# Four-head logit bursts, softmax normalisation in token layout, and an instruction order from a list scheduler, in a two-layer attention and feed-forward kernel

## The chip, the cores and the metric

The kernel runs on one core of a Trainium2 chip. The metric is the device time of one execution in microseconds (us). A run more than 1.5% above the fastest of its kernel counts as slow.

The engines are PE (matrix multiply; PEld is its weight load), DVE (vector), ACT (activation), POOL (general purpose) and SP (here only a queue that issues DMAs). "PEclk" is the TensorE clock that the throttle granted, as a share of full speed.

## The reference, cut to what matters

```python
def _A_ref(x, wq, wk, wv, wo, beta):        # S 2048, D 512, H 32 heads of Dh 16, N 4 segments of L 512
    ...                                      # q, k, v per head and segment
    phi = lambda t: jnp.where(t > 0, t + 1.0, jnp.exp(t))
    g = _sigmoid(beta).reshape(1, H, 1, 1)
    for s in range(N):
        logits = einsum('bhqd,bhkd->bhqk', qs, ks) * scale + mask      # causal inside the segment
        a_dot = einsum('bhqk,bhkd->bhqd', softmax(logits), vs)
        pq = phi(qs)
        a_mem = einsum('bhld,bhde->bhle', pq, M) / (einsum('bhld,bhd->bhl', pq, z)[..., None] + 1e-06)
        outs.append(g * a_mem + (1.0 - g) * a_dot)
        pk = phi(ks)
        M = M + einsum('bhld,bhle->bhde', pk, vs);  z = z + einsum('bhld->bhd', pk)
    ...
    return o @ wo

def _B_ref(x, w1, w3, w2):                   # F = 1376
    return (silu(x @ w1) * (x @ w3)) @ w2

x = x + _A_ref(layernorm(x), ...);  x = x + _B_ref(layernorm(x), ...)      # twice, the same weights
```

With 16 channels a head, the logits use only a small part of the PE's rows, so several heads are run side by side in row groups ("row-tiled"); the products with V are run side by side in column groups ("column-tiled"); projections and the feed-forward part (FFN) use the full array. Changing from one form to another is called a mode change below.

## The kernel before

A small scheduler orders the instructions of each engine ahead of time with durations that the author wrote down; the order in the program is then fixed, and engines wait for each other by semaphores. It takes, engine by engine, the instruction that can start earliest, with program order breaking ties. Program order itself interleaves attention with "fillers", the FFN of the previous segment:

```python
# schedule(): among the pending operations of engine e
if cand is None or ready < cand_ready - 1e-9:
    cand, cand_ready = op, ready
if ready <= tf + 1e-9:
    break
# ... cut ...
def run_interleaved(main_gen, ratio=2):
    for _ in main_gen:                     # one quad (four heads) of attention,
        for _r in range(ratio):            # then two pieces of FFN
            if fillers: ...
```

Logits are computed for two heads at a time, two exponentials per unit, and the value product follows each unit:

```python
for ui, blocks in enumerate(QUNITS):       # 3 units for each quad of heads
    for half in range(2):
        pgs = (2 * half, 2 * half + 1)     # two row groups of four
        # lg_fn: for each block and each pg of pgs: one 32-row matmul
        S.add("pe", lg_fn, ..., writes=hres)
        S.add("act", ... Ebuf[:, 2*half:2*half+2, 0:NT_] = exp(Sl4[:, 2*half:2*half+2, 0:NT_]))
    # pool: affine_select masks; pe: ad_fn, the value product, column-tiled, into ONE bank Xb
```

The output of each quad is channel-major in PSUM. DVE transposes it, and the memory term, out of PSUM, and normalises there; then transposes the whole back:

```python
S.add("dve", ... e.transpose(ST[:, 0], Xb[:, 0:512]))        # attention
S.add("dve", ... e.transpose(ST[:, 1], Yb[:, 0:512]))        # memory, from the nd4 matmuls
... reciprocals, gates ...
otb = ST0 * r0;  oslot = ST1 * r1;  oslot += otb             # three DVE products, 256 columns each
S.add("dve", ... e.transpose(oT[0][:, G, :], ost))           # back, once for two quads
```

The softmax here doesn't subtract the row's maximum and nothing guards it: scores larger than these inputs give would overflow.

## Time and profile before

728.47 us median of 4 runs (727.32 to 729.45). The profiled run has a span of 726.4 us.

| before | PE | DVE | ACT | POOL | idle PE | granted clock |
|---|---|---|---|---|---|---|
| whole span, 726.4 us | 582.2 | 527.7 | 444.7 | 206.5 | 144.2 | 0.908 |
| 160 to 480 us | 264.9 | 237.7 | 201.0 | 90.5 | 55.1 | 0.93 |

The page's busy line, then PE's busy tenths in 40 slices of 18.2 us and the granted clock in tenths, then the chain of work that ended last, by engine:

```profile
PE 582.2 (80%) x4192; PEld 203.4 (28%) x4192; DVE 527.7 (73%) x1178; ACT 444.7 (61%) x586; POOL 206.5 (28%) x292
...
PE   0776897889958888788958899588987898988497
...
PEclk9986569899979999899988999789998999899889
...
PE 41%; DVE 37%; ACT 8%; DMA 6%; issue 4%; SPq 2%; POOL 1%; POOLq 0%; DVEq 0%
```

No engine is full, and the chain passes from PE to DVE and back: it is a kernel in which engines wait for each other. The timeline of PE in the middle shows how (start, duration, engine and line, operation, in the brackets the idle time before it and what ended it). L531 is logits, L553 values, L565 the memory read, L678 and L682 the FFN:

```profile
231.30 0.40 PE L553 MATMUL psall<-Ebuf,Vaug 128*32 128x512 bf16 x4 [0.55 <-DVE ST L575]
231.65 0.34 PE L531 MATMUL psall<-qT,kTm_0 32*128 32x256 bf16 x4
231.92 1.04 PE L682 MATMUL psall<-xnT,w 128*128 128x512 bf16 x4
232.79 1.03 PE L678 MATMUL psall<-xnT,w 128*128 128x512 bf16 x4
233.75 0.35 PE L553 MATMUL psall<-Ebuf,Vaug 128*32 128x384 bf16 x4
...
234.97 0.40 PE L565 MATMUL psall<-phiQ,Maug 32*32 32x512 bf16 x4 [0.54 <-DVE ST L578]
235.30 0.39 PE L531 MATMUL psall<-qT,kTm_1 32*128 32x512 bf16 x2
236.14 1.04 PE L682 MATMUL psall<-xnT,w 128*128 128x512 bf16 x4 [0.46 <-DVE pb L687]
```

Each burst is short, the modes alternate (687 mode changes in the built order), and small waits for DVE are spread between them.

The last view has three stretches of 8 us and one of 30: from and to, length, busy time of PE, PEld, DVE, ACT and POOL with their instructions, granted clock, DMA share, GB/s. In the two stretches where PE is busy 40% and 37% of the time the clock is 0.55 and 0.50, and where it is busy 81% the clock is 1.00. But from 75 to 105 us PE is busy 89% and the clock is 0.50 all the same:

```profile
200.00:208.00 8.00, 3.20 (x25) 0.74 (x26) 7.90 (x16) 4.71 (x5) 3.98 (x4) 0.55 0.39 80
232.00:240.00 8.00, 6.45 (x54) 2.27 (x55) 6.33 (x15) 6.12 (x9) 2.58 (x4) 1.00 0.00 0
376.00:384.00 8.00, 2.96 (x18) 0.84 (x19) 1.72 (x4) 3.48 (x5) 2.70 (x5) 0.50 0.48 98
75.00:105.00 30.00, 26.84 (x179) 6.14 (x180) 13.54 (x28) 26.80 (x35) 14.23 (x23) 0.50 0.00 1
```

The Trainium skill ("TensorE: Matmul & The Clock Gate", Part 1) says that an idle PE is granted half speed and gets full speed after about 3.4 us of sustained work. This trace agrees as to the two levels: 0.50 and 0.55 in the dry stretches, 1.00 in the dense one. It does not agree as to the time: the clock stays at half from 75 to 105 us with PE busy for 26.8 of these 30 us, from 78.48 to 82.88 us without a pause.

### The profile page before, as it was taken

The page shows a single profiled execution, that of the slowest core. Times are in us where ns is not written, and L with a number is a line of the kernel's source. Part 1 is how long each engine was busy: PE and PEld are TensorE (multiplying, and loading weights), DVE is VectorE, ACT ScalarE, POOL GpSimd, SP SyncE. Part 2 cuts the span into 40 slices and gives each one's busy share as a digit, 9 for nine tenths or more (in the row PEclk, how much of TensorE's full clock was granted, in tenths as well). Part 3 has the DMA queues.
Part 4 walks back from the last instruction along what each step waited for, and adds up shares of the span by engine and source line. Part 5 has one row for each costly group of instructions (what it writes and reads, how often), then busy time and mean ns, then how long its engine had stood idle before and what let it go on. Part 6 is the DMA issues. An engine that isn't in the chain of part 4 may idle for free.

```text
span 726.4 us, 10730 instructions
## 1 busy us (share of the span) xinstructions
PE 582.2 (80%) x4192; PEld 203.4 (28%) x4192; DVE 527.7 (73%) x1178; ACT 444.7 (61%) x586; POOL 206.5 (28%) x292
## 2 busy tenths in 40 slices
PE   0776897889958888788958899588987898988497
PEld 0221222223312333223312233122332232223143
DVE  7647468978777778977865677777778869877654
ACT  0658989674657757677475846567476764675020
POOL 3314443331233323232321312223223233222000
PEclk9986569899979999899988999789998999899889
DMA  5933001300040000300021000300012001000200
GB/s 174 289 89 59 1 1 29 59 1 1 1 85 4 1 1 8 81 1 1 0 51 39 0 1 6 80 5 1 1 37 52 1 1 45 15 1 1 54 4 30
DMA packets 56931, 23.81 MB, mean 33 GB/s; under 512 B 52544, under 2 KB 55120, under 8 KB 56880
## 3 DMA queue, kind: packets, MB, share of 16 engines
q1 hardware_dynamic: 54912, 15.22, 9.9%
q0 software_dynamic: 1968, 7.91, 3.3%
q8 instruction: 33, 0.54, 0.3%
q14 instruction: 18, 0.15, 0.1%
HBM read 8.43 MB, written 2.10 MB: 14 GB/s over the span
## 4 chain that ended last, share of the span: by engine, by line
PE 41%; DVE 37%; ACT 8%; DMA 6%; issue 4%; SPq 2%; POOL 1%; POOLq 0%; DVEq 0%
PE psall L678 8%; PE psall L682 8%; PE psall L701 8%; DMA xnT<-xn 5%; ACT Ebuf L539 5%; DVE ST L575 5%; DVE pb L687 4%; PE psall L553 4%; PE psall L531 4%; PE psall L628 3%; DVE ST L578 3%; DVE hT L690 3%; DVE ostage L617 2%; DVE phiK L491 2%; DVE otmp L611 2%
## 5 line engine op out<-in xcount | busy, mean ns | idle before, releaser
L539 ACT ACTIVATE Ebuf<-psall 128x768 bf16<-128x768 f32 (+1 forms) x384 | 317.4, 885 | 66.7 <-PE psall L531 66.2
L544 POOL TENSOR_SCALAR_AFFINE_SELECT Ebuf<-Ebuf 128x512 bf16<-128x512 bf16 x256 | 180.0, 704 | 385.7 <-ACT Ebuf L539 381.3
L685 ACT ACTIVATE sgb<-psall 128x512 bf16<-128x512 f32 (+1 forms) x88 | 52.5, 597 | 111.4 <-PE psall L678 111.4
L678 PE MATMUL psall<-xnT,w 128*128 128x512 bf16 (+1 forms) x352 | 99.7, 409 | 18.0 <-DMA xnT<-xn 17.6
L682 PE MATMUL psall<-xnT,w 128*128 128x512 bf16 (+1 forms) x352 | 102.6, 408 | 6.3 <-DVE pb L687 5.2
L575 DVE STREAM_TRANSPOSE ST<-psall 128x512 f32<-128x512 f32 x64 | 45.6, 712 | 72.5 <-PE psall L553 72.4
L553 PE MATMUL psall<-Ebuf,Vaug 128*32 128x512 bf16 (+3 forms) x1024 | 75.8, 333 | 19.0 <-DVE ST L575 14.8
L687 DVE SCALAR_TENSOR_TENSOR pb<-sgb,psall 128x512 bf16<-128x512 bf16 (+1 forms) x88 | 58.6, 665 | 35.3 <-PE psall L682 20.0
L701 PE MATMUL psall<-w,hT 128*128 128x512 bf16 (+1 forms) x352 | 81.0, 380 | 2.0 <-DVE x_tok L705 1.5
L531 PE MATMUL psall<-qT,kTm_1 32*128 32x128 bf16 (+3 forms) x512 | 65.4, 332 | 9.4 <-ACT Ebuf L539 9.2
L531 PE MATMUL psall<-qT,kTm_0 32*128 32x256 bf16 (+3 forms) x512 | 63.4, 330 | 10.3 <-ACT Ebuf L539 10.0
L690 DVE TENSOR_TENSOR hT<-pb,psall 128x512 bf16<-128x512 bf16 (+1 forms) x88 | 59.7, 678 | 1.0
L466 ACT ACTIVATE qT<-psall 128x512 bf16<-128x512 f32 x32 | 19.3, 603 | 63.3 <-PE psall L450 63.3
L450 PE MATMUL psall<-xnT,wq 128*128 128x512 bf16 x128 | 36.3, 403 | 26.3 <-DMA xnT<-xn 26.0
L678 PEld LDWEIGHTS psall<-xnT,w 128*128 128x128 bf16 (+1 forms) x352 | 33.4, 104 | 68.1 <-DMA xnT<-xn 19.5
L682 PEld LDWEIGHTS psall<-xnT,w 128*128 128x128 bf16 (+1 forms) x352 | 31.5, 105 | 53.2 <-DVE pb L687 16.6
L565 PE MATMUL psall<-phiQ,Maug 32*32 32x512 bf16 x192 | 21.3, 435 | 31.2 <-DVE ST L578 25.4
L553 PEld LDWEIGHTS psall<-Ebuf,Vaug 128*32 128x32 bf16 x1024 | 21.0, 95 | 87.8 <-issue 43.8
L701 PEld LDWEIGHTS psall<-w,hT 128*128 128x128 bf16 (+1 forms) x352 | 32.5, 98 | 44.2 <-DVE x_tok L705 5.4
L628 PE MATMUL psall<-wo,oT 128*128 128x512 bf16 x128 | 37.4, 402 | 8.6 <-DVE oT L620 5.2
L427 DVE TENSOR_SCALAR xn<-x_tok,lnmv 128x512 bf16<-128x512 bf16 x64 | 28.2, 475 | 21.2 <-DMA xnT<-xn 17.3
L416 DVE BATCH_NORM_STATS2 lnst<-x_tok 128x6 f32<-128x512 bf16 x64 | 42.0, 674 | 0.3
(72 smaller groups left out, 604.7 us busy)
## 6 DMA issues: line engine op xcount, KB each, us to landing
w<-in_B_w_dram POOLq DMA_DIRECT2D x2, 1376.0 KB, 13.1
out_dram<-x_tok SPq DMA_DIRECT2D x4, 512.0 KB, 2.9
x_tok<-in_A_x_dram POOLq DMA_DIRECT2D x3, 512.0 KB, 7.0
w<-in_B_w_dram POOLq DMA_DIRECT2D x1, 1280.0 KB, 17.6
xnT<-xn SPq DMA_TRANSPOSE x64, 2.5
x_tok<-in_A_x_dram SPq DMA_DIRECT2D x4, 128.0 KB, 2.9
wq<-in_A_wq_dram POOLq DMA_DIRECT2D x1, 512.0 KB, 4.7
wk<-in_A_wk_dram POOLq DMA_DIRECT2D x1, 512.0 KB, 5.6
```

Of the source, the lines that this page charges most:

```text
L531: ins = e.matmul(Sl4[:, pg, ecol:ecol + N], kTm[sp][ee][32 * pg:32 * pg + 32, G, 128 * j:128 * j + 128], qT[sp][32 * pg:32 * pg + 32, G, 1 ...
L539: S.add("act", lambda e, eslot=eslot, NT_=NT_, half=half: e.activation(Ebuf[eslot][:, 2 * half:2 * half + 2, 0:NT_], Sl4[:, 2 * half:2 * h ...
L544: S.add("pool", lambda e, eslot=eslot, ecol=ecol: e.affine_select(Ebuf[eslot][:, :, ecol:ecol + 128], Ebuf[eslot][:, :, ecol:ecol + 128], ...
L553: ins = e.matmul(Xb[32 * pg:32 * pg + 32, 128 * j:512], Vaug[sp][:, j, heads[pg], :], Ebuf[eslot][:, pg, ecol:ecol + N], start=(j == 0), s ...
L575: S.add("dve", lambda e, ST=ST: e.transpose(ST[:, 0, :, :].rearrange("p a r -> p (a r)"), Xb[:, 0:512]), reads=[xres], writes=[("ST", sts, ...
L628: S.add("pe", lambda e, i=i, G=G, pso=pso: e.matmul(pso, oT[0][:, G, 128 * i:128 * (i + 1)], wo_sb[:, G, :], start=(G == 0), stop=(G == NC ...
L678: S.add("pe", lambda e, cg=cg, f0=f0, fw=fw, gps=gps, b=b: e.matmul(gps[0:fw, :], w1_sb[:, cg, f0:f0 + fw], xnT[b][:, cg, :], start=(cg == ...
L682: S.add("pe", lambda e, cg=cg, f0=f0, fw=fw, ups=ups, b=b: e.matmul(ups[0:fw, :], w3_sb[:, cg, f0:f0 + fw], xnT[b][:, cg, :], start=(cg == ...
L685: S.add("act", lambda e, k3=k3, fw=fw, gps=gps: e.activation(sgb[k3][0:fw, :], gps[0:fw, :], ACT.Tanh, scale=0.5), reads=[gres], writes=[( ...
L687: S.add("dve", lambda e, k3=k3, fw=fw, ups=ups: e.scalar_tensor_tensor(pb[k3][0:fw, :], sgb[k3][0:fw, :], 1.0, ups[0:fw, :], ALU.add, ALU. ...
L690: S.add("dve", lambda e, k3=k3, fw=fw, ft=ft, gps=gps: e.tensor_tensor(hT[0:fw, ft, :], pb[k3][0:fw, :], gps[0:fw, :], ALU.mult), reads=[( ...
L701: S.add("pe", lambda e, ft=ft, fw=fw, i=i, dps=dps: e.matmul(dps[:, :], hT[0:fw, ft, 128 * i:128 * (i + 1)], w2_sb[0:fw, ft, :], start=(ft ...
```

## The change

The intent: take work off PE and DVE, and find a better order. The whole kernel is rewritten on a new scheduler. In its core (cut):

```diff
 # scheduler
-    earliest ready operation of the engine, program order breaks ties
+    lim = max(smin, tf) + LOOK[e]                  # all that can start within LOOK ns (pe 90, act 150, dve 40)
+    for s, op in cands:
+        if s > lim: continue
+        pr = op.prio
+        if e == "pe" and op.mode == "C":           # "PE modes": C = value products, F = full array
+            pr = 1e5 + pr if pe_mode == "F" and s - op.avail_at < C_AGE else -1e5 + pr
+        if pick is None or (pr, s, op.seq) < pick[0]:
+            pick = ((pr, s, op.seq), s, op)
+    buffer slots are no longer fixed in the program: Pool/Buf, given out when an operation is picked

 # attention
-    for half in range(2):  two row groups, one exp of 1024 or 768 columns
+    UNITS of 4 x 512 columns:   for pg in range(4): one 32-row matmul    # four heads at once, all four S banks
+    act:  exp of 2048 columns, one instruction                            # the ONE logit slot
-    value product after every unit (three bursts)
+    value product once for each quad (one burst of 16 matmuls)
+    HP = -1e6:  prio of logits, exp, masks, values;  fillers have their segment number

 # normalisation
-    DVE transposes PSUM -> ST, normalise in f32, three products, DVE transpose back
+    ev:   ACT or DVE (the scheduler chooses) copies the quad PSUM -> xs, bf16
+    dmaT: xs -> xg, token layout, on SP's queue;  DVE: rd, t2 (POOL may take it), oadd
+    dmaT: og -> ot

 # memory
-    column-tiled update and 32-row read, masked per parity
+    full-array matmuls against a block-diagonal memory (mb = macc * bdm)

 # loads
-    DVE:  w2 = 0.5 * w2   (one operation of 5120 columns)
+    POOL: w2 = 0.5 * w2   (two operations of 2560 columns)
```

## The prediction

> **What bounds the kernel now.** No engine is full. The page gives PE busy 582 us (80%), DVE 528 (73%), ACT 445 (61%) of 726; the chain that ended last is PE 41%, DVE 37%, ACT 8%, DMA 6%. The stretches of time show a start (0 to 40 us, PE busy 14), an interleaved middle (105 to 640 us: PE 448 of 535, DVE 411, ACT 350) and the last FFN alone (from 684 us). The timeline shows PE chopped into bursts: 2 row-tiled logit matmuls, 4 column-tiled value matmuls, 4 to 8 full ones. Consecutive bursts of different modes start about 0.1 us further apart than their columns need (0.35 us behind a 512-column one). The Trainium skill, "TensorEngine Tiling (Array Packing)", Key Properties, says that changing the tiling mode drains the engine; this trace agrees, at 0.1 us.
>
> **What changes** (counts from the built program, durations from this trace; estimates).
> - PE: logits use four row groups at once instead of two: 68 to 34 us of columns at full clock. Mode changes fall from 687 to 427, about -26 us. Memory read and update become full-array matmuls, 17 to 24 us. Full matmuls (1568 x 0.216 = 338) and values (34) stay. Sum about 475 at full clock, 520 at a granted 0.91; 582 before.
> - DVE: out go 112 PSUM transposes (79 us), 32 output transposes (22), the otmp/ostage products (73), small reciprocal and gate operations (59). In come 110 PSUM evictions at 0.68 (75), 37 products (17), 24 memory products (16), 24 adds (10), about 32 of small ones; phi and key masks fall by 23. Group sums overcount busy time by 9% today; corrected, 528 to about 420.
> - ACT: 160 exps of 2048 at about 1.87 (299 us, 324 now); evictions 57 to 31; 445 to about 400.
> - POOL: 256 masks stay (180); products and w2 halving join: 207 to about 235.
> - DMA transposes: 96 to 184. On SP's queue they follow at 1.28 us: about 236 us, no limit, but 2.5 us of latency twice in each output path.
>
> **How much is critical.** The built order is regular: one logit burst, 8 to 11 full matmuls, until 80 us of PE work without attention remain. There is one logit slot: exp 1.87 plus 0.6 for release, mode change and matmul, so 160 x 2.5 = 400 us by ACT; in that part DVE needs about 390, PE 395/0.92 = 430. Three nearly equal engines in fixed order lose 7 to 12%: about 470 us. Start about 28, tail about 90 (with one exposed normalisation and its transposes). **Predicted 588 us, 80% range 555 to 636. Faster by over 2%: 0.95; within: 0.035; slower: 0.015.**
>
> **What would show it.** PE busy near 85% of a shorter span; DVE busy 400 to 450, ACT 390 to 420; exp mean 1.8 to 1.95 us; ACT idle about 0.5 us before exps, released by logits; SP's transposes 1.3 us apart; in the chain more PE, less DVE.
>
> **What could be wrong.** A lower granted clock in the first segment (0.50 between 75 and 105 us now); two-port DVE operations and POOL masks blocking each other (the skill's "SBUF — State Buffer", Who interferes with whom, calls it an exclusive lock; no view here isolates it); transposes queued behind weight loads at the start (a 16 us gap now); an order built on wrong durations, leaving every engine waiting.

## The result, and the profile after

562.63 us median of 4 runs (560.59 to 563.92) against 728.47. The ratio is 0.7719 (95% interval 0.7700 to 0.7737), 22.8% less. Ratios here and below are the mean time of one kernel's fast runs over that of the other's of the same rounds, so they are not quite the ratios of the medians.

The same three views of the changed kernel, its page's busy line, PE's tenths and the clock's in slices of 14.0 us, the chain:

```profile
PE 484.8 (86%) x3836; PEld 198.4 (35%) x3904; DVE 445.5 (79%) x893; ACT 395.5 (71%) x324; POOL 235.2 (42%) x326
...
PE   1837568758999899999989999999999999989897
...
PEclk9956789877999899999999999999999999999999
...
PE 48%; DVE 24%; DMA 11%; issue 7%; ACT 4%; POOL 4%; SPq 1%; POOLq 0%
```

PE's idle time is 560.7 - 484.8 = 75.9 us; it was 144.2. So of the 165.7 us saved in the span, 97.4 are PE busy time and 68.3 are waits. Not all of the 97.4 is work that no longer exists, since the same matmul is shorter at a higher clock: busy time times the mean clock of the span gives an estimated 529 and 458 us at full clock, so about 70 us are work and the rest is clock. (68 of 3904 matmul records are missing in this trace, so the busy part is a little too large and the waits too small; a later trace of almost the same kernel, complete, has PE busy 489.9.) The granted clock rose from 0.908 to 0.945.

Where the PE work went is in the groups by line. These sums overlap each other, because ends of matmuls are modelled, so only differences are read. First before, then after (busy us, mean ns, idle time just before, and what ended it):

```profile
L553 PE MATMUL psall<-Ebuf,Vaug 128*32 128x512 bf16 (+3 forms) x1024 | 75.8, 333 | 19.0 <-DVE ST L575 14.8
L531 PE MATMUL psall<-qT,kTm_1 32*128 32x128 bf16 (+3 forms) x512 | 65.4, 332 | 9.4 <-ACT Ebuf L539 9.2
L531 PE MATMUL psall<-qT,kTm_0 32*128 32x256 bf16 (+3 forms) x512 | 63.4, 330 | 10.3 <-ACT Ebuf L539 10.0
```

```profile
L682 ACT ACTIVATE e<-psall 128x2048 bf16<-128x2048 f32 x160 | 300.3, 1877 | 57.5 <-PE psall L674 55.1
...
L674 PE MATMUL psall<-q,km 32*128 32x512 bf16 (+3 forms) x1024 | 66.1, 313 | 16.0 <-ACT e L682 14.6
...
L700 PE MATMUL psall<-e,va 128*32 128x512 bf16 (+3 forms) x1024 | 49.2, 316 | 6.2 <-POOL e L685 5.4
```

The 1024 logit matmuls are the same in number and nearly in mean length; side by side in fours instead of twos they take 66 us of PE instead of 116 (the two groups before, 65.4 and 63.4, overlap each other: together their line covers 116.4 us). The value products in bursts of 16 take 49 instead of 76, and no longer wait 15 us for a DVE transpose to free their bank. The exponential's 57.5 us of idle time over 160 instructions is 0.36 each.

The timeline of PE at a similar place (L674 logits, L791 and L543 full array):

```profile
238.23 0.40 PE L674 MATMUL psall<-q,km 32*128 32x384 bf16 x8 [0.26 <-ACT e L682]
238.56 0.60 PE L791 MATMUL psall<-w,h 128*128 128x512 bf16 x2
239.00 1.03 PE L543 MATMUL psall<-xa,wq 128*128 128x512 bf16 x4
239.86 1.03 PE L791 MATMUL psall<-w,h 128*128 128x512 bf16 x4
240.82 0.40 PE L674 MATMUL psall<-q,km 32*128 32x256 bf16 x8
241.15 0.82 PE L791 MATMUL psall<-w,h 128*128 128x512 bf16 x3
241.81 1.03 PE L543 MATMUL psall<-xa,wk 128*128 128x512 bf16 x4
...
243.44 0.40 PE L674 MATMUL psall<-q,km 32*128 32x512 bf16 x4
```

Every 2.6 us or so one logit burst, right when the exponential before it ends, and full-array matmuls between: almost no brackets. And the two stretches, before 160 us and after (busy us of PE, PEld, DVE, ACT, POOL, then clock, DMA share, GB/s):

```profile
0.00:160.00 160.00, 106.42 (x865) 40.16 (x879) 116.96 (x235) 105.83 (x83) 84.04 (x103) 0.82 0.40 99
160.00:480.00 320.00, 305.91 (x2609) 124.77 (x2656) 276.35 (x563) 274.26 (x219) 146.21 (x217) 0.99 0.26 50
```

From 160 to 480 us PE is busy 96% at a clock of 0.99; 53.6 of the 75.9 us of PE's idle time lie before 160 us, at 0.82. The steady part is PE-bound; what is left to win besides PE work is at the start.

### The profile page after: what moved, and what is told of

Its sections match the earlier page's. It is cut to its first block, busy times and chain, and to the rows that moved or that the text cites. A ratio compares the mean times of both kernels' runs of the same rounds, so it can differ in the third digit from the quotient of the medians.

```text
span 560.7 us, 9831 instructions
## 1 busy us (share of the span) xinstructions
PE 484.8 (86%) x3836; PEld 198.4 (35%) x3904; DVE 445.5 (79%) x893; ACT 395.5 (71%) x324; POOL 235.2 (42%) x326
## 4 chain that ended last, share of the span: by engine, by line
PE 48%; DVE 24%; DMA 11%; issue 7%; ACT 4%; POOL 4%; SPq 1%; POOLq 0%
PE psall L767 19%; PE psall L543 6%; PE psall L791 6%; DMA xg<-xs 5%; PE psall L674 5%; PE psall L700 5%; DVE xn L515 4%; ACT e L682 3%; PE psall L743 3%; PE psall L538 3%; DVE ln L502 2%; DMA ot<-og 2%; DMA pkt<-pk 1%; DVE x_tok L746 1%; DMA xf<-xn 1%
## 5 line engine op out<-in xcount | busy, mean ns | idle before, releaser
L682 ACT ACTIVATE e<-psall 128x2048 bf16<-128x2048 f32 x160 | 300.3, 1877 | 57.5 <-PE psall L674 55.1
L685 POOL TENSOR_SCALAR_AFFINE_SELECT e<-e 128x512 bf16<-128x512 bf16 x256 | 168.3, 675 | 205.7 <-ACT e L682 205.6
L767 PE MATMUL psall<-xf,w 128*128 128x512 bf16 (+1 forms) x678 | 172.5, 386 | 9.8 <-DMA xf<-xn 3.3
L767 PEld LDWEIGHTS psall<-xf,w 128*128 128x128 bf16 (+1 forms) x704 | 65.4, 101 | 90.1 <-issue 18.4
L775 ACT ACTIVATE th<-psall 128x512 bf16<-128x512 f32 (+1 forms) x88 | 52.0, 597 | 54.6 <-PE psall L767 54.5
L791 PE MATMUL psall<-w,h 128*128 128x512 bf16 (+1 forms) x334 | 87.2, 380 | 1.3 <-issue 0.8
L674 PE MATMUL psall<-q,km 32*128 32x512 bf16 (+3 forms) x1024 | 66.1, 313 | 16.0 <-ACT e L682 14.6
L777 DVE SCALAR_TENSOR_TENSOR gp<-th,psall 128x512 bf16<-128x512 bf16 (+1 forms) x88 | 59.1, 678 | 18.0 <-ACT th L775 17.4
L783 DVE TENSOR_TENSOR h<-gp,psall 128x512 bf16<-128x512 bf16 (+1 forms) x88 | 59.4, 678 | 9.2 <-PE psall L767 8.6
L700 PE MATMUL psall<-e,va 128*32 128x512 bf16 (+3 forms) x1024 | 49.2, 316 | 6.2 <-POOL e L685 5.4
L515 DVE TENSOR_SCALAR xn<-x_tok,ln 128x512 bf16<-128x512 bf16 x64 | 43.6, 713 | 12.2 <-POOL ln L509 7.6
L538 PE MATMUL psall<-wv,xa 128*128 128x512 bf16 x123 | 37.4, 418 | 14.6 <-DMA xa<-xn 13.7
L791 PEld LDWEIGHTS psall<-w,h 128*128 128x128 bf16 (+1 forms) x352 | 32.1, 98 | 38.1 <-issue 6.6
L674 PEld LDWEIGHTS psall<-q,km 32*128 32x128 bf16 x1024 | 18.0, 93 | 77.0 <-ACT e L682 66.0
L543 PE MATMUL psall<-xa,wk 128*128 128x512 bf16 x120 | 37.6, 404 | 6.8 <-DVE q L441 5.6
L543 PE MATMUL psall<-xa,wq 128*128 128x512 bf16 x123 | 34.2, 382 | 1.8 <-DVE va L441 1.1
L724 POOL TENSOR_TENSOR og<-xg,rd 128x256 bf16<-128x256 bf16 x27 | 20.4, 757 | 28.7 <-DVE rd L718 14.1
L796 DVE TENSOR_TENSOR x_tok<-psall,x_tok 128x512 bf16<-128x512 f32 x32 | 21.9, 684 | 13.2 <-PE psall L791 13.1
```

The source lines that it names most:

```text
L515: dve(lambda e, i=i, tt=tt, xn=xn: e.tensor_scalar(xn_r[xn.slot][:], x_tok[:, tt, :], ln_r[st.slot][:, i, 6:7], ln_r[st.slot][:, i, 9:10], ...
L538: fn = lambda e, cg=cg, G=G, B=B, st=st, sp_=sp_: e.matmul(bank(B), xa_r[X.slot][:, cg, 128 * G:128 * G + 128], wv_sb[:, cg, :], start=st, ...
L543: fn = lambda e, cg=cg, G=G, B=B, st=st, sp_=sp_, w=w: e.matmul(bank(B), w[:, cg, 128 * G:128 * G + 128], xa_r[X.slot][:, cg, :], start=st ...
L674: o = e.matmul(S4[:, pg, c:c + n], km_r[z.km.slot][32 * pg:32 * pg + 32, ee, G, 128 * j:128 * j + 128], q_r[z.q.slot][32 * pg:32 * pg + 32 ...
L682: act(lambda e, N=N, ebuf=ebuf: e.activation(e_r[ebuf.slot][:, :, 0:N], S4[:, :, 0:N], ACT.Exp, scale=SCALE), 4 * N, reads=[(sbuf_, 0)], w ...
L685: pool(lambda e, ebuf=ebuf, c=c: e.affine_select(e_r[ebuf.slot][:, :, c:c + 128], e_r[ebuf.slot][:, :, c:c + 128], pattern=[[0, 4], [1, 128]],
```

## The experiments

The theory after the result had three parts, each a rival to the others as the main cause. (A) Four heads in a burst: less PE time for logits, fewer mode changes. (B) The order: the single logit slot is refilled the moment the exponential ends, and full-array work is spread to fill all the rest. (C) The relief of DVE: the transposes moved from DVE to the DMA queue. All runs below gave the reference's numbers unless said otherwise, and every ratio is against the kernel before, run in the same job.

| run | us, median | ratio, 95% interval |
|---|---|---|
| after_again | 561.41 | 0.7705 (0.7684 to 0.7727) |
| a_half | 635.0 | 0.8648 (0.8620 to 0.8676) |
| a_greedy | 786.85 | 1.0804 (1.0754 to 1.0854) |
| a_dve_load | 562.45 | 0.7723 (0.7687 to 0.7760) |
| b_four | 760.89 | 1.0434 (1.0419 to 1.0450) |
| b_no_st (wrong numbers) | 724.08 | 0.9936 (0.9919 to 0.9952) |
| b_four_no_st (wrong numbers) | 751.3 | 1.0301 (1.0283 to 1.0319) |
| a_attention_first | 596.82 | 0.8174 (0.8144 to 0.8204) |
| b_attention_first | 934.91 | 1.2838 (1.2789 to 1.2887) |
| a_fold | 551.62 | 0.7565 (0.7553 to 0.7576) |
| a_best1 | 550.0 | 0.7542 (0.7520 to 0.7564) |
| a_fold_hold | 541.22 | 0.7417 (0.7389 to 0.7446) |

"a_" marks a variant of the changed kernel, "b_" one of the kernel before.

### after_again: the changed kernel once more

No edit; it is the yardstick.

> The changed kernel unaltered, as the reference for the other runs on this chip. Every theory expects 560 to 565 us and a ratio to before near 0.772.

Measured: 561.41 us, 0.7705. The result repeats.

### a_half: the changed kernel with two heads in a burst

```diff
-    mkpool("S", 1)
+    mkpool("S", 2)                       # two slots of two banks
-    lg: for pg in range(4);  exp of 2048 columns
+    for half in range(2):
+        lg: for pg in (2*half, 2*half+1);  exp of 1024 columns
```

> The changed kernel with its four-head logit bursts undone: two heads per burst and per exp (1024 columns), two logit slots of two banks as before; all else kept, list scheduler rerun. Theory 1 (PE column time, mode changes and ACT's fixed cost per exp are what the bursts save): PE gets about 34 us of columns and 180 more mode changes (about 18 us), ACT 160 more fixed costs of 0.18 us (about 29 us); the span rises by 30 to 60 us, to 592 to 622. Rival (the gain is elsewhere, and two slots hide the 0.35 us that ACT waits for each logit burst now): within 2% of 562.

Measured: 0.8648, which over after_again's 0.7705 is 12.2% longer. Two of its four runs were slow, the profiled one too (span 638.1); the ratio uses the two fast ones, both 630.1. The built order has 607 mode changes instead of 427. The busy line and the groups of the profiled run:

```profile
PE 561.7 (88%) x3835; PEld 212.7 (33%) x3904; DVE 448.4 (70%) x897; ACT 401.9 (63%) x480; POOL 231.6 (36%) x326
...
L686 ACT ACTIVATE e<-psall 128x1024 bf16<-128x1024 f32 x320 | 304.7, 1040 | 49.7 <-PE psall L678 46.6 <-PE psall L705 2.7
```

```profile
L678 PE MATMUL psall<-q,km 32*128 32x384 bf16 (+3 forms) x1024 | 127.9, 323 | 13.7 <-ACT e L686 11.9 <-issue 0.5 <-DVE gp L782 0.3
```

The logits' group is back at 127.9 us of PE (116.4 before the change); PE is busy 561.7 (88%) and is 67% of the chain that ended last. So theory A holds inside the new order, and it holds by PE: 62 us of logit columns, and 180 more mode changes. ACT shows nearly nothing: 320 exponentials of 1.040 us would be 333 us one after the other, but they take 304.7 of ACT against 300.3 for the 160 long ones, since neighbours overlap. So an account in which the long exponential pays by saving ACT the fixed time of 160 instructions fails. (This profile is of a slow run, so its PE times are a little too long; the ACT durations hardly depend on the TensorE clock: 1.026 us for the same 1024 columns before the change.)

The two fast runs are 630.1 - 561.4 = 69 us longer, more than the 30 to 60 us of theory 1, although the 29 us that it gave to ACT did not come. In the profiled run PE is idle for 638.1 - 561.7 = 76.4 us, hardly more than in after_again (558.3 - 483.4 = 74.9), so the difference is PE busy time: the logits' group grew by 62 us, 180 mode changes at 0.10 to 0.14 us would be an estimated 18 to 25 more, and the clock is lower (0.906 here, 0.916 and 0.924 in the fast runs, 0.951 in after_again). Groups overlap, so these do not simply add up, and the run does not separate them. (The drain on a mode change is what the Trainium skill, "TensorEngine Tiling (Array Packing)", Key Properties, says. In the timelines above it is seen where a burst of 512 columns that should take 0.215 us, a quarter of the 0.86 us between two runs of four matmuls at 239.00 and 239.86, is followed 0.33 us later by another mode: 238.23 to 238.56.)

### a_greedy: the same operations in earliest-ready order

```diff
-LOOK = {"pe": 90.0, "act": 150.0, "dve": 40.0, "pool": 20.0, "sp": 20.0}
+LOOK = {"pe": 0.0, "act": 0.0, "dve": 0.0, "pool": 0.0, "sp": 0.0}
-                    pr = op.prio
+                    pr = 0.0             # and the PE-mode branch switched off
```

> The changed kernel's own operations, but the list scheduler without priorities and without lookahead: each engine takes the operation that can start first, ties in program order. Theory (priorities keep logits first and spread the FFN evenly between them): 590 to 630 us, with PE idle in stretches with little FFN work and a longer tail of FFN. Rival (operations and buffers matter, order does not): within 2% of 562.

Measured: 786.85 us, 40% longer than after_again, and 8.0% longer than the kernel before. PE is busy 546.4 (70%), clock 0.781. The waits view (engine, line, what it waited for, us in total, times, longest) shows what fell apart:

```profile
PE psall L674 <- ACT e L682: 136.3, 96, 2.7
...
ACT e L682 <- PE psall L674: 107.9, 111, 11.1
```

In the changed kernel the same two were 14.6 and 55.1 us (in its groups above). The timeline shows both ends of the loss, PE first and then ACT:

```profile
299.79 1.89 PE L743 MATMUL psall<-wo,ot 128*128 128x512 bf16 x8
301.62 0.39 PE L674 MATMUL psall<-q,km 32*128 32x512 bf16 x4
...
309.31 0.61 PE L674 MATMUL psall<-q,km 32*128 32x512 bf16 x4 [2.31 <-ACT e L682]
```

```profile
302.06 1.88 ACT L682 ACTIVATE e<-psall 128x2048 bf16<-128x2048 f32 x1 [2.69 <-PE psall L674]
```

The last eight of a run of projection matmuls that were ready earlier go ahead of a logit burst, and ACT stands idle 2.69 us. Soon after, that work is used up, and PE stands idle 2.31 us in front of the next burst, whose slot ACT still reads. So two orders of the same operations lie 225 us apart: theory B is the largest lever measured here, and the prediction had no term for it. (The scheduler also gives out buffers and chooses the engine of some copies and products, so these differ a little too.) The loss is waits, 786.0 - 546.4 = 239.6 us instead of 74.9, and clock: PE is busy 63 us longer with the same matmuls, at 0.781 instead of 0.951. It is not mode changes: a rebuild of this order has 265 of them, fewer than the 427 of the changed kernel. Both branches of the expectation missed; the order matters far more than it said.

The 225 us are not the order's share of the 166 us that the change saved. Without its priorities the new program falls back on its program order, which has each segment's FFN in one block behind its attention, while the kernel before interleaved the two by hand (`run_interleaved`). No run has the new operations in the old interleaving.

### a_dve_load: put DVE's relief back

```diff
+                for _ in range(1 if oms is None else 2):     # 112 in all, the PSUM transposes' number and size
+                    sx = new("sx")
+                    dve(lambda e: e.transpose(sx_r[sx.slot][:], xs_r[xs.slot][:]), 512, ...)
```

The added transposes write a buffer that nobody reads. The scheduler knows of them.

> The changed kernel with 112 extra DVE transposes of 128x512 bf16 into a scratch tile that nothing reads, at the priority of the softmax operations: about 77 us of DVE work, near what the removed PSUM transposes cost before. Theory 2 (DVE was a bound and its relief is a main part of the gain; it is at 445 of 561 us now, 35 of 40 in the middle): the span rises by 40 to 75 us, to 600 to 637. Rival (PE and the logit loop bound it, DVE has 115 us of slack): rises by less than 15 us, below 577.

Measured: 562.45, the same as after_again (0.7723 against 0.7705, the intervals overlap). The 112 transposes last 0.69 us each, 77 us one after the other; DVE's busy time, in which neighbours overlap, rises by 53 us, and the span does not move:

```profile
PE 483.1 (86%) x3838; PEld 199.0 (36%) x3904; DVE 498.8 (89%) x1003; ACT 393.2 (70%) x320; POOL 236.7 (42%) x332
```

Theory C, as a statement on DVE's load, falls (the added transposes hold no PSUM bank and nothing waits for their result, so their place in the chain is not tested here): at 79% DVE is not what bounds the changed kernel, and at 89% not yet. In its chain DVE's share rises from 24% to 40% without a change in time, which warns that the chain's shares are not what an engine costs.

### b_four, b_no_st, b_four_no_st: the parts in the old kernel

b_four gives the old kernel the four-head burst and one exponential for it, order as the old scheduler makes it:

```diff
-    for half in range(2):  lg of two pgs;  exp of 2*NT_ columns
+    lg of four pgs;  exp of 4*NT_ columns
```

b_no_st cuts the 112 PSUM transposes of DVE from 512 to 32 columns (the rest of ST is preset to 1, so the numbers are wrong):

```diff
-    e.transpose(ST[:, 0, :, :].rearrange("p a r -> p (a r)"), Xb[:, 0:512])
+    e.transpose(ST[:, 0, 0, :], Xb[:, 0:32])
```

b_four_no_st does both.

> The kernel before with one part of the change alone: one four-head logit burst and one exp per unit (2048, 1536, 1536 columns) in place of two halves; its own scheduler. Theory 1 (bursts by themselves carry the gain): PE loses 34 us of columns, ACT 192 fixed costs: 670 to 700 us. Rival (in this kernel PE and ACT wait for the single value bank, the DVE transposes and one logit slot, so fewer columns are not felt; the second slot is lost): 712 to 745 us.

> The kernel before with its 112 PSUM transposes on DVE cut from 512 to 32 columns; numbers are wrong on purpose. DVE loses about 60 to 70 us of work and the value and memory banks come free about 0.55 us earlier. Theory 2 (DVE and the bank it holds bound the kernel before): 650 to 690 us. Rival (PE bursts and mode changes bound it): 712 us or more.

> Both of the former edits in the kernel before; numbers wrong on purpose. If the two savings are independent, the ratios of the two runs multiply. If each hides the other (PE and DVE in one loop, each waiting for the other), both together save clearly more than the two alone: under 640 us.

Measured: b_four 4.3% slower than before; b_no_st 0.6% faster, with DVE busy 480.9 instead of 527.7; both 3.0% slower, where the product of the two alone would be 3.7%. So 47 us less of DVE is worth about 5 us, and it does not unlock the burst either. b_four is slower than both branches of its expectation had it. What it loses is in its waits; the same wait in before, then in b_four:

```profile
ACT Ebuf L539 <- PE psall L531: 66.2, 79, 4.6
...
ACT Ebuf L535 <- PE psall L527: 116.8, 96, 5.4
```

With two halves, PE can compute one half's logits while ACT reads the other; with one burst over all four banks it can not, so ACT waits for logits (before 96 of its 192 exponentials by this view) for as long as the order has put something in front. PE's busy time did fall, 582.2 to 555.8. The four-head burst is a trade of overlap for PE time: it lost in the old order and gained in the new one, which refills the slot at once.

### a_attention_first and b_attention_first: which part of the order

In the changed kernel, keep only the class of attention work ahead of all else, and let everything else be earliest first:

```diff
-                    pr = op.prio
+                    pr = op.prio if op.prio < -1e5 else 0.0
```

In the old kernel, give the old scheduler the look-ahead and the same class rule:

```diff
+FIRST = ("lg", "exp", "mask", "ad_", "nd4", "sttr")
-    earliest ready
+    among those ready within LOOK of the earliest: FIRST before the rest, then earliest
```

> The changed kernel's operations with only the first part of the priorities kept: logits, exps, masks, values and the x and first weight loads first, small lookahead kept; everything else (projections, FFN, memory) earliest first, ties in program order. The plain greedy order took 787 us. If what matters is that a free logit slot is refilled at once: within 4% of 562 us (below 585). If the spreading of the FFN over the attention also matters: 600 to 700.

> The kernel before with the same idea: its scheduler takes logits, exps, masks, value and memory matmuls and their transposes first among operations that could start within the lookahead of the changed kernel, else as before. If order alone is what the kernel before lacked: 640 to 700 us. If it is bound by its fixed banks and by two-head bursts as well: within 3% of 728 us.

Measured: a_attention_first 596.82 us, between the two branches of its expectation. Of the 225 us between a_greedy and after_again, 190 come from this one rule with its look-ahead, and the other 35 from all other priorities (the segment numbers that spread the rest, and copies out of PSUM put ahead). Both belong to theory B.

b_attention_first is 28% slower than before, which neither branch of its expectation had: the old kernel with that rule takes 934.91 us, at a clock of 0.784. POOL's busy tenths (86% of its work is masks, so it shows where attention is) tell how:

```profile
POOL 4344304300034101345003200034100350012000
```

Attention now comes in dense stretches, with stretches between that have none: it runs ahead of its segment's fillers, and they are left over, with nothing to be interleaved with. There each FFN piece waits for its own chain through ACT and DVE (in the groups, 60.6 us of PE's idle time before one FFN line is released by DVE's FFN product). So the rule is not good in itself; something has to ration the fillers. In the changed kernel the priorities by segment number and the slots handed out by the scheduler can do that; that these make the difference is my reading, not a test. I did not run the old kernel with both the rule and the four-head burst, and the token layout was never tried alone; what it contributes by itself (it frees banks and makes the memory products full-array) stays open, and so does the part of the buffers that are now given out freely.

### a_fold: the halving of w2 taken away

In the changed kernel two POOL operations halve w2, and the normalisation on DVE stops meanwhile. Timeline of DVE, then of POOL, in the changed kernel:

```profile
50.44 6.29 DVE L515 TENSOR_SCALAR xn<-x_tok,ln 128x512 bf16<-128x512 bf16 x1
...
58.48 6.74 DVE L515 TENSOR_SCALAR xn<-x_tok,ln 128x512 bf16<-128x512 bf16 x1
```

```profile
49.90 6.68 POOL L485 TENSOR_SCALAR w<-w 128x2560 bf16<-128x2560 bf16 x1
...
58.42 6.66 POOL L485 TENSOR_SCALAR w<-w 128x2560 bf16<-128x2560 bf16 x1
```

A DVE operation whose median is 0.41 us takes about as long as the POOL operation beside it, twice. The Trainium skill ("SBUF — State Buffer", Who interferes with whom) describes this: DVE in its two-port modes and POOL share a pair of ports, and whoever issues first has it for the whole instruction while the other blocks. The trace agrees (no view shows the mode itself): both times POOL began first, by 0.54 and 0.06 us, and DVE was done 0.15 and 0.14 us after POOL. What it cost PE is seen in its timeline, where it waits for a copy that stood behind the second of them on DVE:

```profile
65.88 1.89 PE L543 MATMUL psall<-xa,wk 128*128 128x512 bf16 x4 [5.57 <-DVE q L441]
```

The edit folds the factor into an operation that is there anyway:

```diff
-        pool(... w2_sb = w2_sb * 0.5 ...)                       # three operations, gone
-                dve(... e.tensor_tensor(h, gp, bank, ALU.mult))
+                dve(... e.scalar_tensor_tensor(h, gp, 0.5, bank, ALU.mult, ALU.mult))
```

> The changed kernel without the halving of w2 on POOL; the factor 0.5 goes into the product that makes h, as a scalar-tensor-tensor of equal size. In the profile after, the two 6.7 us POOL operations (at 49.9 and 58.4 us) cover exactly two DVE normalisations that take 6.2 and 6.7 us in place of 0.45. Theory (a DVE operation in a two-port mode is shut out for the length of a POOL operation, and both lie on the chain): no normalisation over 1.5 us, span 8 to 14 us shorter, 549 to 555. Rival (the start is bound by loads and transposes anyway): less than 4 us.

Measured: 551.62 us, 10 less than after_again, inside the expectation. The normalisation's mean fell from 713 to 477 ns, 43.6 to 28.8 us in all. By 160 us it has started 47 exponentials instead of 43; four of them at the later pace of 2.75 us are 11 us, so the gain is won at the start and kept to the end. (The edit also takes the halving off POOL, where masks stood behind it. Between 48 and 70 us PE's waits for POOL in the changed kernel are under 1 us, so that is hardly where the gain comes from.)

### a_best1: the start, by lighter loads

One large wait of a_fold near the start is for a transposed tile of the memory update, which is under way together with the weight loads. The last bracket of this PE timeline of a_fold shows it:

```profile
30.53 0.61 PE L669 MATMUL psall<-q,km 32*128 32x384 bf16 x8 [0.75 <-ACT e L677]
39.47 1.08 PE L589 MATMUL psall<-va,pkt 128*128 128x136 bf16 x8 [8.32 <-DMA pkt<-pk]
```

a_best1 is a_fold with x and the FFN weights loaded in pieces, each started by a value burst of the first segment, and one memset moved from POOL to DVE:

```diff
-        late_loads: x, w1, w3, w2 whole, as soon as the first normalised tile is there
+                if g == 0:                              # after value burst n of the first segment
+                    load_x(2 + n, [(xs, 0)])  for n in (0, 1);   load_w(n - 2, [(xs, 0)])  for n >= 2
```

> The version without the w2 halving (552 us), with the FFN weights and the last x tiles loaded in pieces of 0.35 to 0.75 MB, one behind each value group of the first segment, in place of all at once at 20 us; and the clearing of the value tiles on DVE in place of POOL. In the run without the halving PE waited 8.3 us at 31 us for a memory transpose behind the loads, ACT 8.1 us with it. Theory (the loads delay the transposes, and the in-order PE passes it on to the logits): that wait falls under 2 us, span 538 to 547. Rival (later waits take its place): 548 or more.

Measured: 550.0 us, within 0.3% of a_fold, so the rival's figure. The wait was mended, and the time did not follow. The same place now:

```profile
31.77 1.09 PE L597 MATMUL psall<-va,pkt 128*128 128x136 bf16 x8 [2.08 <-DMA pkt<-pk]
```

In the first 60 us PE is busy 37.3 instead of 33.0, but from 60 to 130 us it is busy 48.9 instead of 51.5, at a lower clock (0.73 up to 105 us and 0.59 after, 0.85 and 0.66 in a_fold). The gain is given back in another dry stretch before 130 us. The delayed loads now fall in it (DMA share 0.49 instead of 0.28 from 60 to 105 us); whether they make it dry I did not test.

### a_fold_hold: make the PE-mode rule bite

In the changed kernel the rule that should let value bursts wait for full-array work adds plus or minus 1e5 to a priority of about -1e6 (the lowest goes first), so it never puts a value burst behind a filler. A build with that branch switched off has the identical order on every engine; the "PE modes" of the change do nothing. This edit, on top of a_fold, makes the rule effective, and lets it hold a burst for up to 4 us instead of 2.5:

```diff
-C_AGE = 2500.0
+C_AGE = 4000.0
-                            pr = 1e5 + pr
+                            pr = 1e7 + pr
```

> The version without the w2 halving, with the scheduler's mode preference made to work: in the changed kernel the value bursts' priority is about -1e6 and the hold adds 1e5 to it, so they still come before every full matmul and the built order is the same with and without the hold. Here the hold adds 1e7 and lasts up to 4 us: value bursts stand beside a logit burst, and the mode changes on PE fall from 427 to 378. Theory (each mode change costs about 0.1 us and PE is the bound): 549 of them less is 5 us, 544 to 549 us in place of 552. Rival (values come later, exp tiles stay held and ACT waits more): 551 or more.

(A slip in that text: "549 of them less" was meant to say 49, the difference of 427 and 378 mode changes.)

Measured: 541.22 us (540.02 to 542.06), 0.7417. This is the best version here, 25.8% below the kernel before and 10.4 us below a_fold, which is about double the 5 us expected; a_fold ran in another job, so the ratios are what to compare, and their intervals are far apart.

```profile
PE 475.4 (88%) x3837; PEld 199.0 (37%) x3904; DVE 442.9 (82%) x912; ACT 387.1 (72%) x310; POOL 216.5 (40%) x318
```

49 mode changes at 0.10 to 0.14 us are 5 to 7 us. The rest has a trace but no proof: the last logit burst starts at 470.3 us in this kernel and at 468.3 in a_fold, while after 480 us only 248 matmul records remain instead of 287. So attention is no faster, and more of the FFN has been done beside it: 39 matmuls at 0.215 us are about 8 us. That is near what fewer mode changes free, but whether it is the cause was not isolated.

## Why the prediction was right, point by point

- **Time.** 588 predicted, range 555 to 636; measured 562.6, inside it. "Faster" had 0.95.
- **The parts.** The sum was a start of 28, a middle of 470 and a tail of 90. In the trace the first exponential starts at 20.5 us, the last one ends at 481.8, and the span at 560.7: 20.5, 461 and 79. Each term was a little too large, by 7, 9 and 11 us. The middle was right for a partly wrong reason. It was built as a uniform 430 us of PE at 0.92 clock, with 7 to 12% lost between "three nearly equal engines". Measured, PE is busy 406 us in it and idle 55: the work was put 24 us too high and the waits 15 us too low, so it is in part luck that the sum is only 9 us off. The first 43 exponentials come every 3.3 us at a clock of 0.79 and the other 117 every 2.75 us at 0.99. The uniform clock averaged a slow start and an undisturbed rest.
- **Three nearly equal engines.** This step fails. DVE was counted as one of three near-limits; a_dve_load shows that 53 us more of DVE busy time cost nothing. From 160 us on, PE alone is near full (96%).
- **PE.** 475 us at full clock, 520 at 0.91, about 85% busy. Measured 484.8 (489.9 in the complete trace of a_fold) at 0.945, 86%. 475/0.945 is an estimated 503, so about half of the miss is the clock. The memory products were 17 to 24 and are 21.9 (28.7 before, by groups). The halving of logit columns is confirmed by a_half: 127.9 us in pairs, 66.1 in fours.
- **DVE, ACT, POOL.** Predicted about 420 (400 to 450), about 400 (390 to 420), about 235. Measured 445.5, 395.5, 235.2. The exponentials fell from 317.4 to 300.3, not from 324: the two shapes summed apart counted their overlap.
- **Exponentials.** Mean 1.877 us (1.8 to 1.95 predicted), idle time before each 0.36 us (0.5 predicted).
- **Named risks.** The POOL and DVE lock did occur (6.3 and 6.7 us) and cost about 10 us, as a_fold shows. A transpose queued behind weight loads did occur (8.3 us in a_fold), but a_best1 shows that it cost nothing lasting. The low clock in the first segment occurred, in the third and fourth slices (5 and 6 tenths). The fourth risk, an order built on wrong durations that leaves every engine waiting, did not, in the steady part.
- **What was missing.** The prediction treated the order as given ("regular") and named no gain for it. a_greedy and a_attention_first show that with the new instructions the order decides between 787 and 561 us. The prediction came out right because it read a good built order as it was; its sums of work are those of a_greedy as well, which has the same operations.
- **DVE's moved transposes.** The prediction listed them as the largest block of DVE savings. b_no_st took 47 us of it away from the old kernel, which was worth 0.6%; a_dve_load put 53 us of DVE busy time into the new one, which cost nothing measurable.

## What to carry to other kernels

A larger burst that uses all of a buffer saves PE time but gives up overlap; count on the saving only if the order lets the buffer be refilled at once: here the same burst made one kernel 4% slower and another 11% faster. When a fixed order is made ahead of time, try the same instructions in another order before moving any work between engines: here two orders of the same operations were 225 us apart, and removing 47 us from a 73% busy engine gained about 5. Check that a scheduling rule changes the order at all, by building with and without it: the one rule that did nothing was worth 10 us once its weight was large enough to act and its time limit was raised.

## What the Trainium skill lacked or had wrong

- "TensorEngine Tiling (Array Packing)", Key Properties, says that a mode change drains the engine but gives no time. The traces here put bursts of different modes 0.10 to 0.14 us further apart than their columns need.
- "DMA: Bandwidth & Descriptors", Rules for kernel authors, says that a transpose next to ordinary DMAs needs nothing. That is on correctness, and the page gives no time for this case. Transposes land in 2.4 to 2.5 us here (medians); in a_fold one issued at 29.7 us beside the weight loads landed after 9.3 us, 0.2 us behind the last of the loads, and PE waited 8.3 us.
- "GPSIMD Engine Reference", 4.1 Engine selection, calls POOL about 2 times slower than DVE for two-input operations and roughly at line rate for one input. Here a one-input tensor_scalar of 2560 bf16 columns took 6.67 us on POOL (2.6 ns a column), and one of 5120 columns took 1.484 us on DVE before the change (0.29 ns a column): 9 times.
